# RWKV-7 recurrence feeding a hash-routed expert layer: GpSimd's products on VectorE and ScalarE, one masked read of k's scores, and the loads of decays on GpSimd's queue

## The chip, the cores and the metric

The kernel runs on one core of a Trainium2 chip. The core has five engines with a queue of instructions each: TensorE (PE, matrix products, with PEld for its weight loads), VectorE (DVE), ScalarE (ACT), GpSimd (POOL) and SyncE (SP, which here only issues DMAs). An engine works its queue in order, and an instruction that waits for another engine holds up all that stand behind it. Times are device microseconds of one execution, and the metric is the median of several executions.

## What is computed

A recurrence over 768 steps for 4 batches and 8 heads, with a state of 40 by 40 for each, and then a layer of 8 experts, of which each token uses one, given by its id:

```python
for t in range(S):                       # B=4, H=8, S=768, D=40
    y[:, :, t] = einsum('bhd,bhde->bhe', rt, state)
    Sa = einsum('bhde,bhe->bhd', state, at)
    state = state * wt[:, :, None, :] - einsum('bhd,bhe->bhde', Sa, bt)
    state = state + einsum('bhd,bhe->bhde', vt, kt)
x = y.transpose(0, 2, 1, 3).reshape(3072, 320)
e = token_ids * 2654435761 % 8           # the token's expert
out[token] = maximum(x[token] @ w1[e], 0) @ w2[e]
```

All values are float32.

## The kernel before, in words

**Tiles and ticks.** The recurrence is computed in chunks of C = 64 steps. A tile is one chunk of two batches with all 8 heads (rows 0 to 63 of the 128 partitions are one batch, 64 to 127 the other); there are 12 chunks and 2 pairs of batches, so 24 tiles `u`. Four tiles make a group, for which VectorE inverts small triangular blocks; 2 chunks (4 tiles) make a round of decays, and there are 6 rounds and 6 groups.

The order of work is written out by hand: each step is registered with a time in ticks (`at_tick`), all steps are sorted by it, and TensorE, VectorE, ScalarE and GpSimd get their instructions in that order. A tick is about one tile. Within a tick the steps have the order of the list `STEPS`: r1, at_t, z, c, y, r_t, sd, a, rc, x, s, v_t, r0, u. SP's order is left to the scheduler.

**Preparing a tile** (`tile_a`, at tick `u`). At `u - 1.0` SP loads the running products of the decays, `pl` and `ql`, from `p_rows` and `q_rows` in DRAM (4 DMAs), and the inputs `al` and `kb` (6 DMAs). At `u - 0.3` GpSimd multiplies `at = al * pl` (L371) and `z = kb * ql` for b and for k (L373, two operations). TensorE transposes `at` and `z` (`t_ps`, `z_ps`), ScalarE copies them back, and TensorE makes the scores `a_ps` in two banks of PSUM. Eight ScalarE copies take `a_ps` apart: `pk` (L413, L414) and `no` (L415) are scores of b, `mk` (L420) those of k, and GpSimd multiplies `mk` with the mask `after` in place (L422).

**Inverting a group** (`group_i`). When four tiles have their `pk`, VectorE transposes it to `nb` (L450), makes 31 pairs of an outer product and an addition (`outer` L459, `ub` L462) over three ticks, and transposes the result to `ut` and `ug` (L470, L471).

**Using a tile** (`tile_m`, `tile_s`, `tile_b`, eight ticks behind its preparation). The pieces that matter here: ScalarE and GpSimd fill `um` (GpSimd's half is L495, `ug` times the column `first`); TensorE makes `r_ps`, `c_ps`, `rc_ps`, `s_ps` and `y_ps`; VectorE masks `rc_ps` into `mr` (L603), scales the new state `st` (L625) and writes the output rows `xs` (L642), which GpSimd's queue stores to `x_rows` (L645). `py`, rows of `p_rows` again, is loaded by GpSimd's queue (L525).

**Decays** (`decays`). SP loads a round's w into `pb` (one buffer). VectorE makes running products forwards into `pb` (L277) and backwards into `qb` (L282), then `own`; TensorE exchanges halves with one small product `f_ps` (L293); VectorE makes `ends` and `rends`. GpSimd multiplies `pb` by `rends` (L311) and VectorE `qb` by `ends` (L317), each 128x1280, and SP stores them as `p_rows` and `q_rows`. The first two rounds are made ahead of the first tile; the later ones begin one tick before a group's four tiles are complete.

**Buffers.** `pl`, `al`, `ql`, `kb` have two buffers each, so a load for tile `u` waits until tile `u - 2` is multiplied. The double banks of PSUM (`two_banks`) are two, used in turn by z_ps, c_ps, sd_ps, a_ps, rc_ps, v_ps: `v_ps` gets the one that `a_ps` had, and the next `z_ps` the one that `rc_ps` had.

After the recurrence come the experts, which are not changed. The functions that the change touches:

## Time and profile before

| | |
|---|---|
| median of 3 runs | 925.74 us (922.95 to 933.06) |
| the profiled execution | 921.35 us, of which 919.6 us span |
| TensorE busy | 720.6 us (78%) |
| VectorE busy | 401.9 us (44%) |
| GpSimd busy | 297.2 us (32%) |
| ScalarE busy | 281.5 us (31%) |

The span is the time from the first to the last instruction in the trace. TensorE's clock is granted by the chip; a granted clock of 1.0 is 2.4 GHz, 0.5 is 1.2 GHz, and a number between is a stretch with both. Of an instruction the trace has its start, its duration, and, where the engine was idle before it, how long and what ended the wait.

### The profile page before, as it was taken

What the parts mean: (1) busy time and instruction counts of PE and PEld (TensorE: products, weight loads), DVE (VectorE), ACT (ScalarE), POOL (GpSimd) and SP (SyncE); (2) the same over time, 40 slices, a digit from 0 to 9 for tenths busy, and PEclk for the clock granted to TensorE, in tenths of its full rate; (3) what the DMA queues carried; (4) which work ended last, traced back from release to release, by engine and by line L of the source; (5) the groups of instructions that cost most, each with busy time, mean ns of one, the idle gap of its engine ahead of it and who ended that gap; (6) DMA issues with size and microseconds to landing.
All of it is one profiled execution on the core that took longest, in us unless ns stands there. A gap on an engine that the chain in (4) does not pass through costs nothing.

```text
span 919.6 us, 25403 instructions
## 1 busy us (share of the span) xinstructions
PE 720.6 (78%) x11032; PEld 503.3 (55%) x11032; DVE 401.9 (44%) x807; ACT 281.5 (31%) x634; POOL 297.2 (32%) x354
## 2 busy tenths in 40 slices
PE   0033344996998788989999929999999999999993
PEld 0022233885787677877888823536363636354542
DVE  8333799888856776586693211010110110110100
ACT  0024442664556365665644400000011011010000
POOL 4044434453545456546522232121221203020101
PEclk9985655996779698898998978999999999999997
DMA  4756385554876576653432163222222314130000
GB/s 78 147 103 127 69 166 107 95 130 97 125 129 91 93 114 106 101 111 63 51 75 54 40 220 96 72 93 78 86 88 79 130 38 153 46 113 1 21 8 16
DMA packets 208033, 83.03 MB, mean 90 GB/s; under 512 B 186926, under 2 KB 198191, under 8 KB 207920
## 3 DMA queue, kind: packets, MB, share of 16 engines
q1 hardware_dynamic: 201008, 64.32, 34.7%
q0 software_dynamic: 6912, 17.07, 6.5%
q8 instruction: 87, 1.43, 0.7%
q14 instruction: 26, 0.21, 0.1%
HBM read 65.58 MB, written 17.08 MB: 90 GB/s over the span
## 4 chain that ended last, share of the span: by engine, by line
PE 59%; issue 8%; POOL 6%; DVE 5%; DMA 3%; SPq 2%; ACT 0%; POOLq 0%; DVEq 0%
PE up_ps L831 21%; PE dn_ps L841 15%; PE y_ps L203 4%; PE z_ps L386 2%; PE nc_ps L203 2%; PE r_ps L203 2%; PE c_ps L203 2%; PE s_ps L203 2%; PE rc_ps L203 1%; PE u_ps L203 1%; POOL z L373 1%; POOL um L495 1%; PE t_ps L428 1%; PE xg_ps L821 1%; POOL at L371 1%
## 5 line engine op out<-in xcount | busy, mean ns | idle before, releaser
L831 PE MATMUL up_ps<-xt,w 128*128 128x512 f32 (+1 forms) x384 | 192.2, 631 | 8.6 <-issue 8.1
L841 PE MATMUL dn_ps<-w,ht 128*128 128x320 f32 x512 | 140.0, 434 | 0.0
L831 PEld LDWEIGHTS up_ps<-xt,w 128*128 128x128 f32 (+1 forms) x384 | 62.9, 189 | 133.7 <-issue 132.7
L841 PEld LDWEIGHTS dn_ps<-w,ht 128*128 128x128 f32 x512 | 96.6, 190 | 45.3 <-issue 6.1
L845 POOL DMA_INDIRECT out_dram<-o,idx_all x32 | 32.0, 1001 | 270.6 <-ACT o L844 265.5
L834 DVE TENSOR_SCALAR ht<-up_ps 128x512 f32<-128x512 f32 x32 | 22.1, 692 | 175.1 <-PE up_ps L831 139.2
L462 DVE TENSOR_TENSOR ub<-ub,outer 128x31 f32<-128x31 f32 (+15 forms) x186 | 92.3, 496 | 6.4
L459 DVE TENSOR_TENSOR outer<-ub,nb 128x31 f32<-128x31 f32 (+15 forms) x186 | 80.6, 433 | 4.5
L836 ACT ACTIVATE ht<-up_ps 128x512 f32<-128x512 f32 x32 | 19.1, 597 | 192.5 <-PE up_ps L831 163.0
L823 DVE COPY xt<-xg_ps 128x256 f32<-128x256 f32 x32 | 13.2, 413 | 128.2 <-PE xg_ps L821 128.2
L422 POOL TENSOR_TENSOR mk<-mk,after 128x512 f32<-128x512 f32 x24 | 32.0, 1332 | 112.2 <-ACT mk L420 95.2
L293 PE MATMUL f_ps<-own,partner 128*128 128x40 f32 x12 | 3.9, 424 | 81.4 <-DVE own L291 81.4
L645 POOL DMA_DIRECT2D x_rows<-xs x48 | 25.9, 544 | 116.4 <-DVE xs L642 69.6
L844 ACT COPY o<-dn_ps 128x320 f32<-128x320 f32 x32 | 13.6, 426 | 148.4 <-PE dn_ps L841 148.4
L428 PE MATMUL t_ps<-ident,at 128*104 128x128 f32 x96 | 21.0, 358 | 48.5 <-POOL at L371 48.5
L293 PEld LDWEIGHTS f_ps<-own,partner 128*128 128x128 f32 x12 | 3.0, 310 | 82.2 <-DVE own L291 82.2
L386 PE MATMUL z_ps<-ident,z 128*104 128x128 f32 x192 | 44.5, 401 | 3.9 <-POOL z L373 3.9
L373 POOL TENSOR_TENSOR z<-kb,ql 128x320 f32<-128x320 f32 x48 | 44.3, 941 | 0.0
L816 POOL DMA_INDIRECT xg<-x_rows,src_all x32 | 30.9, 967 | 35.5 <-PE xg_ps L821 18.6
L428 PEld LDWEIGHTS t_ps<-ident,at 128*104 128x104 f32 x96 | 13.0, 165 | 51.4 <-POOL at L371 50.9
L311 POOL TENSOR_TENSOR pb<-pb,rends 128x1280 f32<-128x1280 f32 x6 | 19.6, 3272 | 63.8 <-DVE rends L305 63.8
L386 PEld LDWEIGHTS z_ps<-ident,z 128*104 128x104 f32 x192 | 31.9, 187 | 12.8 <-POOL z L373 11.5
(153 smaller groups left out, 1239.0 us busy)
## 6 DMA issues: line engine op xcount, KB each, us to landing
w<-in_moe_w_dram SPq DMA_DIRECT2D x8, 1280.0 KB
w<-in_moe_w_dram SPq DMA_DIRECT2D x8, 1024.0 KB
ql<-q_rows SPq DMA_DIRECT2D x48, 160.0 KB
pb<-in_w_dram SPq DMA_DIRECT2D x24, 160.0 KB
al<-in_a_dram SPq DMA_DIRECT2D x48, 80.0 KB
kb<-in_b_dram SPq DMA_DIRECT2D x48, 80.0 KB
kb<-in_k_dram SPq DMA_DIRECT2D x48, 80.0 KB
r<-in_r_dram SPq DMA_DIRECT2D x48, 80.0 KB
```

The lines of the kernel that those rows point to most:

```text
L203: nc.tensor.matmul(out_, lhsT=lhsT, rhs=rhs, start=start, stop=stop, skip_group_check=True)
L373: nc.gpsimd.tensor_tensor(heads(x["z"][:, be]), view(x["kb"][:, be]), view(x["q"][:, be]), op=OP.mult)
L386: nc.tensor.transpose(p[0:R, be, hp * P:(hp + 1) * P], x["z"][:, be, hp, :], ident[:])
L422: nc.gpsimd.tensor_tensor(mk, mk, after[:].unsqueeze(1).to_broadcast([P, H, C]), op=OP.mult)
L428: nc.tensor.transpose(p[0:R, hp, :], src[:, hp, 0:R], ident[:])
L459: nc.vector.tensor_tensor(tv, ub[:, 0:j + 1, j:j + 1].to_broadcast([P, j + 1, m]), nb[:, j, j + 1:].unsqueeze(1).to_broadcast([P, j + 1, m ...
L462: nc.vector.tensor_tensor(o, o, tv, op=OP.add)
L645: nc.gpsimd.dma_start(x_rows[r0:r0 + C, :], xs[half(be), :])
L816: nc.gpsimd.indirect_dma_start(out=xg[:], out_offset=None, in_=x_rows[:], in_offset=bass.IndirectOffsetOnAxis(ap=idx, axis=0))
L831: nc.tensor.matmul(p[:], lhsT=w1[0:m, c, f * P:(f + 1) * P], rhs=xt[0:m, c, 0:n], start=(c == 0), stop=(c == 2))
L841: nc.tensor.matmul(p[:], lhsT=ht[:, f, j * P:(j + 1) * P], rhs=w2[:, f, :], start=(f == 0), stop=(f == FP - 1))
L845: st = nc.gpsimd.indirect_dma_start(out=out[:], out_offset=bass.IndirectOffsetOnAxis(ap=idx, axis=0), in_=o[:], in_offset=None, bounds_che ...
```

## The change

The products `at` and `z` of a tile, and the product of `pb` with `rends`, go from GpSimd to VectorE. GpSimd's half of `um` goes to ScalarE, as a copy with a scale. The columns of `a_ps` are arranged so that k's scores lie together for all rows: VectorE then reads them from PSUM, masks them and writes `mk` in one operation, and b's scores need four ScalarE copies instead of six. The loads of `pl` and `ql` are issued by GpSimd instead of SP. A tile's loads are placed at `u - 1.7` instead of `u - 1.0`, its products at `u - 0.7` instead of `u - 0.3`.

```diff
--- before.py
+++ after.py
@@ -308,7 +308,7 @@
         def _():
 
             p = segs(x["pb"])
-            nc.gpsimd.tensor_tensor(p, p, x["rends"][:].unsqueeze(2).to_broadcast([P, SEG, SL, D]), op=OP.mult)
+            nc.vector.tensor_tensor(p, p, x["rends"][:].unsqueeze(2).to_broadcast([P, SEG, SL, D]), op=OP.mult)
             store(0, x["pb"][:])
 
         @then.append
@@ -344,7 +344,7 @@
         ri, rn = divmod(n, RN)
         x = tiles[u]
 
-        @at_tick(u - 1.0)
+        @at_tick(u - 1.7)
         def _():
             x["p"] = pl = work.tile([P, DM], F32, tag="pl", name="pl")
             x["a"] = al = work.tile([P, DM], F32, tag="al", name="al")
@@ -355,22 +355,22 @@
                 return t.rearrange("t (h e) -> t h e", h=H)
             p_rows, q_rows = (d[rn * C:(rn + 1) * C] for d in pq_dram[ri])
             for be in range(2):
-                nc.sync.dma_start(pl[half(be)], of_batches(p_rows, 2 * g + be, 1))
-                nc.sync.dma_start(ql[half(be)], of_batches(q_rows, 2 * g, 2))
+                nc.gpsimd.dma_start(pl[half(be)], of_batches(p_rows, 2 * g + be, 1))
+                nc.gpsimd.dma_start(ql[half(be)], of_batches(q_rows, 2 * g, 2))
             load(lambda be, rows: by_head(al[rows]), a, 2 * g, n * C)
 
             load(lambda be, rows: by_head(kb[rows, be]), b, 2 * g, n * C)
             load(lambda be, rows: by_head(kb[rows, be]), k, 2 * g, n * C, crossed=True)
 
-        @at_tick(u - 0.3)
+        @at_tick(u - 0.7)
         def _():
             x["at"], x["z"] = at_r(u), z_r(u)
 
             def view(t):
                 return t.rearrange("p (hp two e) -> p hp two e", hp=HP, two=2)
-            nc.gpsimd.tensor_tensor(heads(x["at"]), view(x["a"][:]), view(x["p"][:]), op=OP.mult)
+            nc.vector.tensor_tensor(heads(x["at"]), view(x["a"][:]), view(x["p"][:]), op=OP.mult)
             for be in range(2):
-                nc.gpsimd.tensor_tensor(heads(x["z"][:, be]), view(x["kb"][:, be]), view(x["q"][:, be]), op=OP.mult)
+                nc.vector.tensor_tensor(heads(x["z"][:, be]), view(x["kb"][:, be]), view(x["q"][:, be]), op=OP.mult)
 
         @at_tick(u, "at_t")
         def _():
@@ -395,31 +395,26 @@
                 for be in range(2):
                     for i in range(2):
                         for par in range(2):
-                            c0 = (hp * 2 + be) * C
+
+                            c0 = ((i == be) * HP + hp) * C
                             mm(p[half(i), par, c0:c0 + C], x["z_t"][half40(par), be, hp, half(i)],
                                x["at_t"][half40(par), hp, be, :])
-
-            def scores(rows, be, c0, c1):
-
-                return p[rows].rearrange("p two (hp b t) -> p two b hp t", hp=HP, b=2)[:, :, be, :, c0:c1]
-
+            scores = p[:].rearrange("p two (kb hp t) -> p two kb hp t", kb=2, t=C)
+            of_b = scores[:, :, 1]
+
+            x["mk"] = mk = work.tile([P, 2, HP, C], F32, tag="mk", name="mk", bufs=LAG)
+            nc.vector.tensor_tensor(mk[:], scores[:, :, 0], after[:].unsqueeze(1).unsqueeze(1).to_broadcast([P, 2, HP, C]),
+                                    op=OP.mult)
 
             if ti == 0:
                 groups[gi]["pk"] = work.tile([P, GRP, 2, HP, BLK], F32, tag="pk", name="pk", bufs=1)
             pk = groups[gi]["pk"][:, ti]
             x["no"] = no = work.tile([P, 2, HP, BLK], F32, tag="no", name="no", bufs=LAG)
+            nc.scalar.copy(pk, of_b[:, :, :, 0:BLK])
             for be in range(2):
-                top, low = slice(be * C, be * C + BLK), slice(be * C + BLK, (be + 1) * C)
-                nc.scalar.copy(pk[top], scores(top, be, 0, BLK))
-                nc.scalar.copy(pk[low], scores(low, be, BLK, C))
-                nc.scalar.copy(no[top], scores(top, be, BLK, C))
-
-            x["mk"] = mk = work.tile([P, 2, HP, C], F32, tag="mk", name="mk", bufs=LAG)
-            for be in range(2):
-                rows = half(1 - be)
-                nc.scalar.copy(mk[rows], scores(rows, be, 0, C))
-            mk = mk[:].rearrange("p two hp t -> p (two hp) t")
-            nc.gpsimd.tensor_tensor(mk, mk, after[:].unsqueeze(1).to_broadcast([P, H, C]), op=OP.mult)
+                low = slice(be * C + BLK, (be + 1) * C)
+                nc.scalar.copy(pk[low], of_b[low, :, :, BLK:C])
+            nc.scalar.copy(no[:], of_b[:, :, :, BLK:C])
 
     def turn(t, src):
 
@@ -492,8 +487,8 @@
                 low = slice(be * C + BLK, (be + 1) * C)
                 nc.scalar.copy(xi[low, :, 0:BLK], p[low])
             x["um"] = um = work.tile([P, H, C], F32, tag="um", name="um")
-            nc.gpsimd.tensor_scalar(um[:, :, 0:BLK], groups[gi]["ug"][:, ti * H:(ti + 1) * H, :],
-                                    first[:, 0:1], None, op0=OP.mult)
+            nc.scalar.activation(um[:, :, 0:BLK], groups[gi]["ug"][:, ti * H:(ti + 1) * H, :], AF.Copy,
+                                 scale=first[:, 0:1])
 
         @at_tick(t0 - 1, "u")
         def _():
```

How this moves instructions shows at three places. First VectorE, at the program's start, from the second round's `rends` on. Before:

```order
L305 TENSOR_SCALAR rends<-rends 128x160
L317 TENSOR_TENSOR qb<-qb,ends 128x1280
L319 COPY qb<-ends 128x40
L264 TENSOR_SCALAR qb<-pb 128x1280
L265 SCALAR_TENSOR_TENSOR pb,wbad<-qb,pb 128x1280
```

After (at_84 and at_86 are the two buffers of `at`, z_102 and z_104 the first of ten of `z`; `mk` is L406 now):

```order
L311 TENSOR_TENSOR pb<-pb,rends 128x1280
L317 TENSOR_TENSOR qb<-qb,ends 128x1280
L319 COPY qb<-ends 128x40
L371 TENSOR_TENSOR at_84<-al,pl 128x4x2x40
L373 TENSOR_TENSOR z_102<-kb,ql 128x4x2x40 x2
L371 TENSOR_TENSOR at_86<-al,pl 128x4x2x40
L373 TENSOR_TENSOR z_104<-kb,ql 128x4x2x40 x2
L406 TENSOR_TENSOR mk<-a_ps,after 128x512
L371 TENSOR_TENSOR at_84<-al,pl 128x4x2x40
L373 TENSOR_TENSOR z_106<-kb,ql 128x4x2x40 x2
```

The products of tiles 0 and 1 stand directly behind the second round, and those of tile 1 ahead of the mask of tile 0.

Second GpSimd, in two ticks with all kinds of work. Before:

```order
L422 TENSOR_TENSOR mk<-mk,after 128x512
L495 TENSOR_SCALAR um<-ug,first 128x8x32
L371 TENSOR_TENSOR at_84<-al,pl 128x4x2x40
L373 TENSOR_TENSOR z_102<-kb,ql 128x4x2x40 x2
L525 DMA py<-p_rows 64x320 x2
L645 DMA x_rows<-xs 64x320 x2
L422 TENSOR_TENSOR mk<-mk,after 128x512
```

After:

```order
L358 DMA pl<-p_rows 64x320
L359 DMA ql<-q_rows 64x640
L358 DMA pl<-p_rows 64x320
L359 DMA ql<-q_rows 64x640
L520 DMA py<-p_rows 64x320 x2
L640 DMA x_rows<-xs 64x320 x2
```

The arithmetic is gone, and four more DMAs are issued for each tile.

Third VectorE, where a later round of decays meets the start of a group (from the fifth round's `L277` to its `own`; other rows between are the routing of tokens). Before:

```order
L642 SCALAR_TENSOR_TENSOR xs<-y_ps,py 128x320
L277 TENSOR_TENSOR pb<-pb,qb 128x4x40 x2
L282 TENSOR_TENSOR qb<-qb 128x4x40 x4
L743 CAST eidf<-eid 128x24
```

After:

```order
L637 SCALAR_TENSOR_TENSOR xs<-y_ps,py 128x320
L277 TENSOR_TENSOR pb<-pb,qb 128x4x40
L371 TENSOR_TENSOR at_84<-al,pl 128x4x2x40
L373 TENSOR_TENSOR z_106<-kb,ql 128x4x2x40 x2
L277 TENSOR_TENSOR pb<-pb,qb 128x4x40
L282 TENSOR_TENSOR qb<-qb 128x4x40 x4
L406 TENSOR_TENSOR mk<-a_ps,after 128x512
L738 CAST eidf<-eid 128x24
```

`at` and `z` of the next tile and the mask of this one stand in the middle of the decays, ahead of `nb` and `own`.

## Rows read from the trace of the kernel before

**Rows 1.** Stretches: length, busy time by engine (instructions), granted clock, DMA share, GB/s.

```profile
54.50:97.00 42.50, 17.91 (x304) 13.51 (x304) 8.00 (x18) 18.26 (x42) 16.64 (x18) 0.67 0.69 134
97.00:143.40 46.40, 20.63 (x343) 16.30 (x343) 44.13 (x78) 18.92 (x46) 19.01 (x17) 0.56 0.61 114
...
170.50:218.60 48.10, 41.53 (x1304) 37.23 (x1302) 43.71 (x97) 34.00 (x77) 24.33 (x31) 0.97 0.70 138
218.60:298.50 79.90, 68.56 (x1699) 60.90 (x1699) 56.05 (x113) 39.72 (x92) 38.88 (x44) 0.78 0.65 104
298.50:376.20 77.70, 64.58 (x1707) 57.65 (x1708) 52.43 (x93) 41.72 (x97) 41.40 (x47) 0.82 0.63 108
376.20:444.40 68.20, 60.76 (x1697) 53.35 (x1694) 45.42 (x81) 41.33 (x92) 38.36 (x46) 0.90 0.46 84
```

The engines stand in the order PE, PEld, DVE, ACT, POOL.

**Rows 2.** Timeline of the first tile: start, duration, engine, line, operation, tiles [idle before].

```profile
54.53 0.85 POOL L371 TENSOR_TENSOR at<-al,pl 128x320 f32<-128x320 f32 x1
...
55.43 1.09 PE L428 MATMUL t_ps<-ident,at 128*104 128x128 f32 x4 [6.01 <-POOL at L371]
...
60.51 0.36 ACT L413 COPY pk<-a_ps 32x256 f32<-32x256 f32 x1 [1.16 <-PE a_ps L203]
...
63.89 1.26 POOL L422 TENSOR_TENSOR mk<-mk,after 128x512 f32<-128x512 f32 x1 [6.87 <-ACT mk L420]
...
65.11 0.86 POOL L371 TENSOR_TENSOR at<-al,pl 128x320 f32<-128x320 f32 x1
```

**Rows 3.** Timeline of VectorE: the output rows of two tiles in turn.

```profile
182.55 0.49 DVE L642 SCALAR_TENSOR_TENSOR xs<-y_ps,py 128x320 f32<-128x320 f32 x1
...
196.62 0.49 DVE L642 SCALAR_TENSOR_TENSOR xs<-y_ps,py 128x320 f32<-128x320 f32 x1
```

**Rows 4.** Timeline of TensorE: three waits, the last one of a round of decays.

```profile
365.26 0.65 PE L428 MATMUL t_ps<-ident,at 128*104 128x128 f32 x4 [1.17 <-POOL at L371]
...
360.84 0.43 PE L540 MATMUL v_ps<-ident,x 64*104 64x64 f32 x8 [0.56 <-ACT mk L420]
...
223.47 0.65 PE L293 MATMUL f_ps<-own,partner 128*128 128x40 f32 x2 [6.96 <-DVE own L291]
```

**Rows 5.** Groups by line, 40 to 540 us: count, busy us, mean ns, idle before.

```profile
L373 POOL TENSOR_TENSOR z<-kb,ql 128x320 f32<-128x320 f32 x48 | 44.3, 941 | 0.0
...
L603 DVE TENSOR_TENSOR mr<-rc_ps,after 128x1024 f32<-128x1024 f32 x24 | 29.3, 1220 | 19.2 <-PE rc_ps L203 19.2
...
L645 POOL DMA_DIRECT2D x_rows<-xs x48 | 25.9, 544 | 116.4 <-DVE xs L642 69.6 <-DVE outer L459 40.8 <-DVE pb L277 6.1
```

**Rows 6.** Timelines of GpSimd and VectorE: the first two rounds of decays.

```profile
20.38 4.05 POOL L311 TENSOR_TENSOR pb<-pb,rends 128x1280 f32<-128x1280 f32 x1 [12.62 <-DVE rends L305]
...
21.61 2.86 DVE L319 COPY qb<-ends 128x40 f32<-128x40 f32 x1
...
50.34 1.48 DVE L317 TENSOR_TENSOR qb<-qb,ends 128x1280 f32<-128x1280 f32 x1
```

**Rows 7.** Timeline: GpSimd's `um`, and VectorE's operation that begins beside it.

```profile
346.77 0.95 POOL L495 TENSOR_SCALAR um<-ug,first 128x256 f32<-128x256 f32 x1
...
346.90 3.50 DVE L459 TENSOR_TENSOR outer<-ub,nb 128x192 f32<-128x192 f32 x1
```

**Rows 8.** Stretches, instructions of L459, then of L462: groups 0, 2 and 5.

```profile
97.00:143.40 46.40, 15.30 (x31) 0.56 0.61 114
...
218.60:288.00 69.40, 12.82 (x31) 0.77 0.64 102
...
444.40:484.70 40.30, 10.89 (x31) 1.00 0.40 62
...
97.00:143.40 46.40, 17.52 (x31) 0.56 0.61 114
...
218.60:288.00 69.40, 16.36 (x31) 0.77 0.64 102
...
444.40:484.70 40.30, 11.51 (x31) 1.00 0.40 62
```

## The prediction

> **What bounds the kernel now.** I read first the busy time by stretch [rows 1], cut where the kernel's own stages begin. What follows 444.4 us, the last ticks and the expert layer, prepares no new tiles, and the change hardly touches it. Before that, three things follow one another.
>
> In the first 54.5 us the decays of two rounds are made, one after the other, and nothing else can start. From 54.5 to 97 us the first tiles are prepared at one per 10.58 us (`at` of tile 0 starts at 54.53, of tile 1 at 65.11 [rows 2]), while every engine is less than half busy. The rows show why: GpSimd makes `at`, TensorE transposes from 55.43, ScalarE's eight copies start at 60.51, GpSimd masks `mk` at 63.89, and only then takes `at` of the next tile, because its queue holds them in that order. It is one serial loop through four engines. From 97 to 143.4 us VectorE is the bound: it is busy 44.13 of 46.4 us with the first group's block inversion [rows 1].
>
> Then the recurrence runs, four tiles to a group, and the three stretches of 79.9, 77.7 and 68.2 us are four ticks each [rows 1]. No engine is full in them: VectorE is busy 56.05 of 79.9 us. TensorE is busy 68.56 us, but at a granted clock of 0.78 (a mixture of its levels 1.2 and 2.4 GHz); 68.56 times 0.78 is 53.5, and the same product is 53.0 and 54.7 in the next two stretches. So about 54 us per group is what TensorE needs at 2.4 GHz, and a good tick shows it: between two `xs` rows, 182.55 and 196.62, lie 14.07 us [rows 3], or 56.3 per group. The other 12 to 24 us per group are TensorE's waits and the lower clock behind them. The waits are of three kinds [rows 4]: at the head of a tile for GpSimd's `at` (1.17 us), before `v_ps` for ScalarE's copies of `mk` out of PSUM (0.56 us), and once per round for VectorE's decays (`f_ps`, 6.96 us).
>
> **The change part by part.** *VectorE's new work.* Per tile it gets one `at`, two `z` and one `mk`. The trace has no such operation on VectorE; the nearest is `xs`, 128x320, 0.49 us [rows 3], and for `mk` from PSUM the masking `mr`, twice as large, 1.22 us [rows 5], so 0.65 with some fixed cost. That is 3 times 0.49 plus 0.65, or 2.1 us per tile (bounds: 1.8, were all priced by size at `mr`'s rate, and 4.0, were the three to cost GpSimd's 0.94 [rows 5] and `mk` as much as `mr`). I take 2.1, since `xs` has the same shape. Per round it also gets the product with `rends`, 128x1280, whose twin `L317` takes 1.48 us [rows 6]. Per group: 4 times 2.1 plus 1.5, or 9.9 us.
>
> *What VectorE gets back.* While GpSimd computes, VectorE stalls: with `um` (and `at` and `z` behind it) on GpSimd from 346.77 us, one 128x192 product took 3.50 us [rows 7], and a 128x40 copy under GpSimd's 4.05 us product took 2.86 us [rows 6]. The block inversion's 62 operations take 15.30 + 17.52 = 32.8 us in group 0 and 12.82 + 16.36 = 29.2 in group 2, but 10.89 + 11.51 = 22.4 in the last group, where no `at`, `z` and `mk` are left [rows 8]. So 10.4 us come back in group 0 and about 7 in a later one. By the Trainium skill ("SBUF — State Buffer", Who interferes with whom) a VectorE instruction with two SBUF inputs and a GpSimd instruction that reads SBUF block one another for whole instructions. The trace agrees in the 3.50 us row, and by that rule all of the stretching ends, since what GpSimd keeps are memsets and DMA issues. Net, a later group costs VectorE some 3 us more: 59, where TensorE needs 56.3.
>
> *Start.* The product with `rends` moves from 4.05 us on GpSimd to 1.48 on VectorE, ahead of `L317`. GpSimd's product of the first round ends at 20.38 + 4.05 = 24.43 now, VectorE's would at 21.86 [rows 6]; so the stores, the next load, which the store must free a buffer for, and the second round move up by 2.6 us. `L317` of that round starts at 50.34 now [rows 6], so VectorE has the two products done at 47.74 + 1.48 + 1.48 = 50.7, and with 0.2 allowed for the copy behind them starts `at` of tile 0 at 50.9 instead of 54.53. Gain: 3.6 us.
>
> *First tiles.* By the order of VectorE, `at` and `z` of tile 1 now stand ahead of `mk` of tile 0, so the loop is cut. A tile then costs what TensorE and ScalarE need in a row: 60.51 less 55.43, or 5.1 us (lower bound 20 us for four); the upper bound is the 42.5 us of now. Between them stands the DMA work of this stretch: 0.69 of 42.5 us is 29 us of all DMA engines [rows 1], and the loads are the same. I take 29. Gain: 13.5 us.
>
> *First group.* 46.4 us, less 10.4 of stalls, plus 1.5 and three tiles at 2.1: 43.8. Gain: 2.6 us.
>
> *From 143.4 to 218.6* an `f_ps` wait stays, since VectorE is as full ahead of it as before, and the ticks behind it, from 170.5 us on, run at a granted clock of 0.97 already [rows 1]. Gain: 0, give or take 4.
>
> *Groups from 218.6 on.* `at` comes about half a tick earlier, on an engine that has time, so the 1.17 us wait ends, and with it the clock loss that follows. What is late next is `f_ps`: on VectorE `nb`, the rest of the decays and `own` stand in line as before, now with `at`, `z` and `mk` ahead of them. I keep 7 us for it and 7 us for the half clock behind it: 56.3 + 14 = 70 in the two groups that hold decays, and 58.5 in the third, which has none. Gains: 10, 7.7 and 9.7 us.
>
> *Costed at nothing.* ScalarE's copies out of `a_ps` fall from eight to four per tile and `um` comes to it; by its busy share of about half in the groups [rows 1] both are covered. Loading `pl` and `ql` from GpSimd takes four of SP's loads per tile away and puts four issues of 0.54 us [rows 5] where GpSimd's arithmetic stood; they start 0.7 tick earlier. Behind them on GpSimd stand `py` and the stores of `x_rows`, both needed a tick later. If that cover fails, rival (d) prices it.
>
> Sum: 3.6 + 13.5 + 2.6 + 0 + 10 + 7.7 + 9.7 = 47.1 us. The profiled execution took 921.35 us (span 919.6), which gives 874.3; the median of the runs, 925.74, is 4.4 higher, which gives 878.7. I say 877, and put the rivals on the same footing, some 2.5 above the profiled execution's.
>
> **The rivals.** (a) *TensorE's floor everywhere*: without GpSimd's stalls VectorE reaches `own` in time, so the 14 us of wait and half clock go in two groups (28 more), the third group gains 2 more, and the first tiles run at 5.1 us each (8.5 more): about 838. For it: VectorE idles over 20 us in each of those stretches. Against: the `f_ps` wait comes from a burst, not from the mean.
>
> (b) *VectorE in order takes most of it back*: `mk` now waits on VectorE for `a_ps`, with the inversion queued behind it, and `v_ps` takes `a_ps`'s PSUM buffer, so a late `mk` holds TensorE. If the later groups keep their 79.9, 77.7 and 68.2 us, only the start's 19.7 us are gained: about 904.
>
> (c) *Slower*: the same hold, but large. If VectorE's lag reaches `v_ps` by some 7 us in every tick, the size of the `f_ps` wait, TensorE falls to half clock each time and all ticks run as in the worst group, 20 us. The three groups then cost 3 times 79.9 less 225.8, or 14 more, and the 48.1 us from 170.5 on, three ticks of 16 us, 12 more; less the start's 19.7, that is 6 slower than now: about 930, and over 1% where the clock stays low between. It decides from a lag of 7 us per tick. Against: VectorE's mean of 59 in 70 us leaves it room to recover.
>
> (d) *No net change, loads late*: GpSimd now issues about ten DMAs per tick. If each had to wait for a VectorE operation, as the copy of 2.86 us waited for GpSimd [rows 6], ten times 0.54 + 2.86 is 34 us per tick, over twice the tick; a third of such waits would already use up the gain: about 923. Against: few VectorE operations are copies. The Trainium skill ("SBUF — State Buffer", SBUF: two separate sides) warns of just this: GpSimd cannot write a DMA's descriptors during a two-port VectorE copy. No row here shows a DMA issue so delayed.
>
> **How the numbers follow.** My forecast 0.47 (858 to 898), (a) 0.15 (830 to 858), (b) 0.22 (898 to 914), (d) 0.08, (c) 0.08. Faster by over 1%, about what a measurement of this kernel can tell from no change, holds the first three: 0.84; within 1% 0.08; slower 0.08. The range 845 to 910 leaves out (c), (d), the best of (a) and the worst of (b); the bounds of VectorE's price, -0.3 and +1.9 us for each of 24 tiles, -7 and +46 were all of it on the path, lie inside it but for the far end.
>
> **What would show it.** After: `at` of tile 1 close behind `z` of tile 0, `nb` of group 0 near 80 us and its last transposition back near 124; inversion operations at some 22 us per group all over; the wait for `at` before `t_ps` gone; ticks of 14 to 15 us in the last full group. Wrong if `v_ps` waits for VectorE's `mk` by over 2 us per tick, if `at` waits for `pl` or `ql`, or if the granted clock in the groups stays at 0.8.

## The result and the profile after

The changed kernel takes 898.94 us (median; 894.51 to 918.71), the kernel before 924.35 beside it: a ratio of 0.969, interval 0.962 to 0.976. The profiled execution took 894.51 us, its span 892.7 instead of 919.6. The forecast of 877 us had the direction and the start, and nearly twice the gain. Of two kernels below (a_noload and b_noload) only one execution of four was undisturbed, so only medians and the lowest times are told of them, and their traces, like that of a_pool_mask, are of disturbed executions. The same stretches as in [rows 1], from the windows of the changed kernel (the columns are those of [rows 1]), cut at the same events (`at` of tile 0, `nb` of group 0, end of the first inversion, first `mr`, `nb` of groups 2 to 5, last `xs`):

```profile
0.00:50.80 50.80, 2.10 (x6) 1.21 (x6) 33.38 (x74) 2.21 (x9) 11.94 (x37) 1.00 0.60 109
50.80:84.20 33.40, 20.30 (x304) 16.77 (x304) 15.51 (x37) 11.68 (x27) 11.40 (x22) 1.00 0.96 189
84.20:123.70 39.50, 20.78 (x343) 17.74 (x343) 37.45 (x91) 11.68 (x30) 4.12 (x8) 0.82 0.76 131
123.70:151.70 28.00, 15.09 (x317) 13.42 (x314) 23.67 (x61) 9.88 (x25) 7.96 (x16) 0.58 0.58 110
151.70:203.60 51.90, 46.88 (x1304) 43.03 (x1302) 42.92 (x109) 27.58 (x63) 13.57 (x26) 0.87 0.55 113
203.60:277.40 73.80, 60.49 (x1699) 55.07 (x1699) 55.78 (x129) 36.21 (x84) 25.05 (x40) 0.88 0.73 119
277.40:349.80 72.40, 62.33 (x1705) 56.73 (x1707) 49.60 (x110) 36.52 (x84) 25.84 (x42) 0.84 0.66 110
349.80:415.90 66.10, 60.09 (x1702) 54.32 (x1699) 42.78 (x94) 36.05 (x80) 24.81 (x38) 0.92 0.51 78
415.90:511.90 96.00, 89.81 (x2680) 82.43 (x2676) 49.04 (x103) 45.06 (x98) 16.09 (x32) 0.91 0.25 49
```

Set against the forecast (us gained; before less after):

| stretch | before | after | gained | forecast |
|---|---|---|---|---|
| to `at` of tile 0 | 54.5 | 50.8 | 3.7 | 3.6 |
| first tiles | 42.5 | 33.4 | 9.1 | 13.5 |
| first group | 46.4 | 39.5 | 6.9 | 2.6 |
| to `nb` of group 2 | 75.2 | 79.9 | -4.7 | 0 |
| three groups | 225.8 | 212.3 | 13.5 | 27.4 |
| to the last `xs` | 91.9 | 96.0 | -4.1 | 0 |
| expert layer | 383.3 | 380.8 | 2.5 | 0 |
| span | 919.6 | 892.7 | 26.9 | 47.1 |

The first three rows sum to 19.7 in both columns, but that agreement is partly luck: the first tiles gained 4.4 less than forecast and the first group 4.3 more. Of the 20.2 us that are missing in the end, 13.9 lie in the three groups and 8.8 in the two stretches around them; the 2.5 of the expert layer, which was not changed, go the other way.

What the forecast asked the trace to show is mostly there. In the timeline of VectorE and ScalarE, `at` of tile 1 stands close behind `z` of tile 0, where [rows 2] had 10.58 us from one `at` to the next; then tile 2 waits for its load:

```profile
50.84 0.48 DVE L371 TENSOR_TENSOR at<-al,pl 128x320 f32<-128x320 f32 x1
51.24 0.89 DVE L373 TENSOR_TENSOR z<-kb,ql 128x320 f32<-128x320 f32 x2
52.05 0.48 DVE L371 TENSOR_TENSOR at<-al,pl 128x320 f32<-128x320 f32 x1
...
57.25 0.69 DVE L406 TENSOR_TENSOR mk<-a_ps,after 128x512 f32<-128x512 f32 x1 [3.92 <-PE a_ps L203]
57.98 0.37 ACT L413 COPY pk<-a_ps 128x256 f32<-128x256 f32 x1 [2.62 <-DVE mk L406]
...
63.70 0.49 DVE L371 TENSOR_TENSOR at<-al,pl 128x320 f32<-128x320 f32 x1 [5.75 <-DMA al<-in_a_dram]
```

`nb` of group 0 stands at 84.2 us (forecast: near 80) and its last transposition ends near 123.7 (near 124). The prices are those of the forecast: 0.48 us for `at`, 0.45 for each `z`, 0.69 for `mk`, 2.06 per tile against the 2.1 taken. The last row but one holds what no step had foreseen: ScalarE's copy of b's scores waits for VectorE's `mk`, since both read the tile `a_ps` and `mk` is written first.

The inversion's operations fall to 21.1 us in every group, 10.5 plus 10.6 (forecast: some 22; [rows 8] had 32.8, 29.2 and 22.4), here grouped by line from 203.6 to 266.5 us:

```profile
L457 DVE TENSOR_TENSOR ub<-ub,outer 128x31 f32<-128x31 f32 (+15 forms) x31 | 10.6, 343 | 1.1
L454 DVE TENSOR_TENSOR outer<-ub,nb 128x31 f32<-128x31 f32 (+15 forms) x31 | 10.5, 340 | 0.6
```

What did not come are ticks of 14 to 15 us all through the last full group: its `mr` rows stand 17.5, 16.2, 15.0 and 17.5 us apart. Of the signs that the forecast named for being wrong, `v_ps` does not wait for `mk`, and `at` waits for `al` and not for `pl` or `ql`; the granted clock in the groups, 0.88, 0.84 and 0.92, rose from 0.78, 0.82 and 0.90, but in the second group little.

**Where the gain of the groups went.** In the three groups TensorE is busy 182.9 of 212.3 us. Busy time times granted clock, row by row, is 160.9 us, and 161.1 before: TensorE's work at full clock, unchanged. The rest is idle time (29.4 now, 31.9 before) and what the half clock costs, busy time less that product (22.0 now, 32.8 before). So the idle time hardly fell; of the 13.5 us gained, 10.8 are half clock. TensorE's waits show why; first the kernel before, 218.6 to 444.4 us, then the changed one, 203.6 to 415.9 (us in total, times, longest):

```profile
PE f_ps L293 <- DVE own L291: 14.2, 2, 7.2
PE t_ps L428 <- POOL at L371: 8.0, 9, 1.4
PE s_ps L203 <- issue: 4.1, 4, 1.4
...
PE z_ps L386 <- POOL z L373: 2.0, 9, 0.3
```

```profile
PE f_ps L293 <- DVE own L291: 11.9, 2, 6.5
PE s_ps L203 <- issue: 4.8, 4, 2.2
PE x_ps L203 <- issue: 4.1, 2, 2.5
PE y_ps L203 <- issue: 3.0, 2, 1.8
...
```

The waits for GpSimd's `at` and `z`, 10 us, are gone as forecast. In their place stand more stops put down to "issue", in which TensorE waits for nothing that the profile shows: 17.3 us in all instead of 9. Most stand in the middle of a stream of equal matmuls, as here (timeline of TensorE):

```profile
169.16 0.54 PE L203 MATMUL u_ps<-ug,xi 32*64 32x32 f32 x12
170.68 0.92 PE L203 MATMUL u_ps<-ug,xi 32*64 32x32 f32 x20 [0.98 <-issue]
...
239.38 0.62 PE L203 MATMUL s_ps<-x,z 128*40 128x40 f32 x21
242.16 0.43 PE L203 MATMUL s_ps<-x,z 128*40 128x40 f32 x11 [2.16 <-issue]
```

Windows cut from the end of one stop to the end of a later one (the first number with an x counts matmuls) give them a pattern:

```profile
165.65:170.67 5.02, 4.04 (x128) 3.55 (x127) 4.85 (x11) 3.30 (x8) 1.55 (x4) 1.00 0.68 178
170.67:186.59 15.92, 14.61 (x381) 13.57 (x382) 10.88 (x35) 8.49 (x19) 4.15 (x8) 0.79 0.46 99
236.95:242.15 5.20, 3.04 (x127) 2.75 (x128) 4.99 (x12) 2.55 (x7) 4.59 (x9) 1.00 1.03 216
242.15:259.08 16.93, 15.25 (x382) 14.04 (x381) 10.16 (x28) 7.91 (x18) 5.53 (x9) 0.80 0.98 141
352.18:380.21 28.03, 25.94 (x637) 23.71 (x637) 17.53 (x45) 14.01 (x30) 7.03 (x11) 0.82 0.58 90
```

The counts are 1, 3, 1, 3 and 5 times 128, less one or a few. With its weight loads a block of 128 matmuls is 256 instructions. Counted so, 15.0 of the 17.3 us lie between two blocks; the rest are shorter stops elsewhere, the longest 0.86 us. The DMA queue of the instructions, in the page of the same kernel, fits that:

```profile
q8 instruction: 87, 1.43, 0.7%
```

These are 87 packets of 16.4 KB, and 11032 matmuls with 11032 weight loads make 86.2 blocks of 256. I read a stop as TensorE having used up one block of instructions before the next is there. The times of these packets bear that out: between 150 and 510 us TensorE makes twelve stops of 0.88 us or more, and each ends 1.32 to 1.62 us after such a packet has landed, where the packets start 5.0 us apart in the mean. Where two stops lie one block apart (165.66, 236.96 and 310.40 us to the next), the packet between them starts 2.5, 2.7 and 1.4 us after the block's first matmul, lands at 3.7, 3.7 and 3.2 us, and TensorE goes on at 5.0, 5.2 and 4.7 us, though it was busy with the block for only 4.0, 3.0 and 2.2 us. The kernel before has the stops too (128 matmuls from 258.92 to 263.84 us, and from 409.34 to 413.81).

The half clock begins mostly behind such stops, or in a wait. Between 150 and 510 us nine stretches at half clock begin, by windows of half a microsecond; seven begin in a stop of 0.88 us or more or up to 2 us behind its end, the other two (205 and 277 us) in the waits for `f_ps`, the first of these 2.2 us behind a stop. Four stops of over 1 us (270.95, 300.09, 342.99 and 380.22 us) were followed by none. Around the stop that ends at 242.16:

```profile
240.00:242.20 2.20, 0.04 (x3) 0.04 (x4) 2.13 (x5) 2.10 (x6) 1.90 (x4) 1.00 1.09 215
242.20:244.20 2.00, 2.00 (x37) 1.71 (x37) 1.92 (x5) 0.70 (x2) 0.89 (x1) 0.66 1.82 187
244.20:246.20 2.00, 2.00 (x38) 1.94 (x38) 1.80 (x6) 0.09 (x1) 0.00 (x0) 0.50 1.06 62
...
248.20:250.20 2.00, 2.00 (x16) 1.77 (x15) 0.00 (x0) 0.78 (x2) 0.00 (x0) 0.64 0.53 59
250.20:252.20 2.00, 2.00 (x80) 1.95 (x81) 0.00 (x0) 1.92 (x4) 0.00 (x0) 1.00 1.05 237
```

TensorE idles 2.2 us, then runs seven at a granted clock of about 0.5, that is at 1.2 GHz, and then is back at 2.4. So this stop of 2.2 us costs some 5.5 us with the half of the seven.

### The profile page after: what moved, and what is told of

Its sections match the earlier page's. It is cut to its first block, busy times and chain, and to the rows that moved or that the text cites. A ratio compares the mean times of both kernels' runs of the same rounds, so it can differ in the third digit from the quotient of the medians.

```text
span 892.7 us, 25236 instructions
## 1 busy us (share of the span) xinstructions
PE 722.1 (81%) x11032; PEld 511.7 (57%) x11032; DVE 392.2 (44%) x909; ACT 249.6 (28%) x562; POOL 204.5 (23%) x324
## 2 busy tenths in 40 slices
DMA packets 204192, 83.02 MB, mean 93 GB/s; under 512 B 186926, under 2 KB 195119, under 8 KB 204080
## 4 chain that ended last, share of the span: by engine, by line
PE 73%; DVE 12%; issue 5%; DMA 5%; SPq 2%; ACT 1%; POOL 0%; DVEq 0%; POOLq 0%
PE up_ps L826 22%; PE dn_ps L836 16%; PE r_ps L203 5%; PE y_ps L203 4%; PE s_ps L203 4%; PE u_ps L203 3%; PE rc_ps L203 3%; PE t_ps L423 3%; PE nc_ps L203 2%; PE a_ps L203 2%; PE z_ps L386 2%; PE c_ps L203 2%; PE sd_ps L648 2%; PE x_ps L203 2%; DVE qb L282 1%
## 5 line engine op out<-in xcount | busy, mean ns | idle before, releaser
L457 DVE TENSOR_TENSOR ub<-ub,outer 128x31 f32<-128x31 f32 (+15 forms) x186 | 63.8, 343 | 6.3
L454 DVE TENSOR_TENSOR outer<-ub,nb 128x31 f32<-128x31 f32 (+15 forms) x186 | 63.2, 340 | 3.8
L203 PE MATMUL a_ps<-at_t,z_t 40*64 40x64 f32 x1536 | 36.4, 247 | 12.7 <-ACT z_t L388 11.1
L637 DVE SCALAR_TENSOR_TENSOR xs<-y_ps,py 128x320 f32<-128x320 f32 x24 | 11.8, 491 | 72.4 <-PE y_ps L203 70.0
L203 PEld LDWEIGHTS a_ps<-at_t,z_t 40*64 40x64 f32 x1536 | 30.8, 156 | 20.2 <-ACT z_t L388 16.2
L358 POOL DMA_DIRECT2D pl<-p_rows x48 | 25.8, 537 | 69.7 <-DVE at L371 43.8
L386 PE MATMUL z_ps<-ident,z 128*104 128x128 f32 x192 | 36.7, 355 | 0.7 <-DVE z L373 0.7
L203 PE MATMUL r_ps<-x,mk 64*64 64x40 f32 x768 | 33.0, 249 | 1.0 <-issue 0.9
L598 DVE TENSOR_TENSOR mr<-rc_ps,after 128x1024 f32<-128x1024 f32 x24 | 29.1, 1215 | 10.3 <-PE rc_ps L203 10.3
```

The source lines that it names most:

```text
L203: nc.tensor.matmul(out_, lhsT=lhsT, rhs=rhs, start=start, stop=stop, skip_group_check=True)
L358: nc.gpsimd.dma_start(pl[half(be)], of_batches(p_rows, 2 * g + be, 1))
L386: nc.tensor.transpose(p[0:R, be, hp * P:(hp + 1) * P], x["z"][:, be, hp, :], ident[:])
L454: nc.vector.tensor_tensor(tv, ub[:, 0:j + 1, j:j + 1].to_broadcast([P, j + 1, m]), nb[:, j, j + 1:].unsqueeze(1).to_broadcast([P, j + 1, m ...
L457: nc.vector.tensor_tensor(o, o, tv, op=OP.add)
L598: nc.vector.tensor_tensor(t[:].rearrange("p two h t -> p (two h) t"), p[:].rearrange("p two (h t) -> p (two h) t", t=C), after[:].unsqueez ...
```

## The experiments

Every ratio is to the kernel before, run on the same chip beside it; the changed kernel's is 0.969 (0.962 to 0.976).

**1. The order alone, on GpSimd (b_order).**

```diff
 # the kernel before
-        @at_tick(u - 1.0)        # loads of a tile
+        @at_tick(u - 1.7)
-        @at_tick(u - 0.3)        # at and z
+        @at_tick(u - 0.7)
```

> The kernel before with two numbers changed: a tile's loads are issued at tick u - 1.7 instead of u - 1.0, and its at and z are made at u - 0.7 instead of u - 0.3. All arithmetic stays on GpSimd, which now makes at and z of the next tile ahead of mk of this one. Theory 'order': the first tiles were slow because GpSimd's queue closed a loop through four engines, so cutting the loop alone gives most of the 9 us that the stretch of the first tiles gained (42.5 to 33.4): 915 us, and nb of group 0 near 88 us instead of 96.9. Theory 'engine': GpSimd's own 4.9 us per tile and its stalls of VectorE are the matter: no change, 922 to 926. In both the 62 inversion operations of group 0 stay near 33 us.

Measured: 928.98 us, ratio 1.001 (0.996 to 1.007). The start does gain: `at` of tile 0 starts at 51.72 and of tile 1 at 54.17, and `nb` of group 0 stands at 89.89 instead of 96.92. By the first `mr` 8.4 us of it are left (162.09 for 170.53), two ticks later none (200.08 for 199.85). The inversion costs VectorE 29 to 34 us in groups 0 to 4, since GpSimd's `at` and `z` still run under it. In the groups TensorE's waits for `at` are gone by the order alone, but its stops are 18.0 us there and its wait for `f_ps` 17.8. Both theories were half right: the order opens the loop, and without the other engine nothing of it reaches the end.

**2. The engine alone, in the old order (a_late).**

```diff
 # the changed kernel
-        @at_tick(u - 1.7)
+        @at_tick(u - 1.0)
-        @at_tick(u - 0.7)
+        @at_tick(u - 0.3)
```

> The changed kernel with the old ticks: loads at u - 1.0, at and z at u - 0.3, so that VectorE makes them behind mk of the tile before and the loop of the first tiles is closed again, with VectorE in GpSimd's place. Theory 'order and engine each bring a part of the start': the first tiles take about 40 us instead of 33, and the groups wait for at as before: 908 to 914. Rival 'the engine alone': VectorE's 2 us per tile instead of GpSimd's 5 keep the loop short, 897 to 902.

Measured: 897.64 us, ratio 0.957 (0.950 to 0.963). The engine alone does it; the interval lies a little below the changed kernel's and all but clear of it, so the new order brings nothing that shows. The waits for `at` in the groups are gone here too, and the stops are 15.0 us. The loop is closed again, as the timeline of VectorE shows, but it takes 7.0 us now:

```profile
57.49 0.48 DVE L371 TENSOR_TENSOR at<-al,pl 128x320 f32<-128x320 f32 x1
...
63.90 0.69 DVE L406 TENSOR_TENSOR mk<-a_ps,after 128x512 f32<-128x512 f32 x1 [5.12 <-PE a_ps L203]
64.51 0.48 DVE L371 TENSOR_TENSOR at<-al,pl 128x320 f32<-128x320 f32 x1
```

That is no longer the bound: `nb` of group 0 stands at 83.05 us, with the loop open at 84.22. By their share, 0.96 in the changed kernel and 0.98 here, the DMA engines bound the stretch in both; no run made its loads lighter.

**3. `at` and `z` back on GpSimd, in the new order (a_pool_atz).**

```diff
-            nc.vector.tensor_tensor(heads(x["at"]), ...)     # and z
+            nc.gpsimd.tensor_tensor(heads(x["at"]), ...)
```

> The changed kernel with at and z back on GpSimd, everything else, the order too, as changed. Theory 'GpSimd stalls VectorE': the inversion operations, 21 us per group now, grow to some 26 us wherever at and z lie under them (groups 0 to 4), the first group's stretch grows by 4 to 5 us and f_ps comes later: about 908. Rival 'VectorE's load counts': VectorE is freed of 1.5 us per tile and at and z have time on GpSimd, so 895 to 899.

Measured: 916.89 us, ratio 0.987 (0.969 to 1.005). This interval touches the changed kernel's, so the times alone leave it open; the trace does not. The start keeps its gain (`nb` of group 0 at 82.50), the three groups lose all of it: 234.2 us instead of 212.3. VectorE's operations grow where the theory had them, to 27.6 us in group 2 (by line, 202.8 to 272.5 us):

```profile
L457 DVE TENSOR_TENSOR ub<-ub,outer 128x31 f32<-128x31 f32 (+15 forms) x31 | 15.8, 509 | 1.1
L454 DVE TENSOR_TENSOR outer<-ub,nb 128x31 f32<-128x31 f32 (+15 forms) x31 | 11.8, 381 | 0.6
```

`f_ps` then waits 9.22 us instead of 5.34 in that group, and 4.92 instead of 6.52 in the next. TensorE idles only 3.3 us more in the three groups; what doubles is its loss to the half clock, 43.8 us for 22.0. So that VectorE's operations stretch under `at` and `z` is shown, and that TensorE loses its clock with it in this one execution; how the one leads to the other is not. The stretching agrees with the rule of the Trainium skill ("SBUF — State Buffer", Who interferes with whom) that the prediction weighed.

**4. The mask back on ScalarE and GpSimd (a_pool_mask).**

```diff
-            nc.vector.tensor_tensor(mk[:], scores[:, :, 0], after..., op=OP.mult)
+            for be in range(2):
+                nc.scalar.copy(mk[half(1 - be)], ...)        # and six copies of pk and no
+            nc.gpsimd.tensor_tensor(mk, mk, after..., op=OP.mult)
```

> The changed kernel with the masking of k's scores as before: ScalarE copies mk out of a_ps in pieces (eight copies per tile again) and GpSimd masks it in place; at, z, um, the product with rends, the ticks and the loads as changed. Theory 'every GpSimd operation that reads SBUF under the inversion costs VectorE': one operation per tile of about 1.3 us instead of the three of at and z, so a third to a half of the 18 us that at and z cost: 905 to 908, the inversion at 23 to 24 us per group. Rival 1: ScalarE's eight copies hold v_ps up too, 912 or more. Rival 2: the copies wait for TensorE alone and not for VectorE, so 890 to 897.

Measured: 918.76 us, ratio 0.972 (0.963 to 0.982), which cannot be told from the changed kernel's. The inversion takes 23.2 us per group with a mask under it, as the theory had it; whether the mask alone is worth time stays open.

**5. `pl` and `ql` by SP's queue (a_spload).**

```diff
-                nc.gpsimd.dma_start(pl[half(be)], ...)       # and ql
+                nc.sync.dma_start(pl[half(be)], ...)
```

> The changed kernel with pl and ql loaded through SP's queue again, at the new tick u - 1.7. Theory 'who issues is indifferent': 895 to 903. Rival 1, 'GpSimd's issues are slow' (its own waits for xs stand ahead of them): faster, 885 to 893. Rival 2, 'on SP's queue they hold up what stands behind them' (SP waits for the stores of p and q there): the first tiles slow down, 905 to 912.

Measured: 908.52 us, ratio 0.971 (0.964 to 0.979), not to be told from the changed kernel's. In the trace `nb` of group 0 stands at 87.68 instead of 84.22: a small part of rival 2, no more.

**6. ScalarE's copies ahead of `mk` (a_swap).**

```diff
-            nc.vector.tensor_tensor(mk[:], ...)              # ahead of the copies
             nc.scalar.copy(pk, ...)                          # and three more
+            nc.vector.tensor_tensor(mk[:], ...)
```

> The changed kernel with mk on VectorE written behind ScalarE's four copies out of a_ps, so that the copies wait for TensorE alone and mk waits for them. Theory 'copies behind mk': ScalarE's 79.3 us of waits for mk hold um, xi and x_t behind them and with them TensorE; then each group gains 2 to 4 us and the whole about 886 to 890, the waits of 'pk' for VectorE being gone. Rival: ScalarE has the time, or VectorE's new wait takes it back: 899 give or take 4.

Measured: 907.63 us, ratio 0.980 (0.963 to 0.997). In the changed kernel ScalarE's waits before `pk` are (40 to 510 us):

```profile
ACT pk L413 <- DVE mk L406: 79.3, 24, 9.4
```

They are gone here and no time with them. The interval is 3.4% wide; it leaves out the 886 to 890 us of the theory by little, and a smaller gain it can't exclude.

**7. `f_ps` later (a_fps).**

```diff
-            p = bank([P, D], "f_ps")                         # at the end of the step that makes own
-            nc.tensor.matmul(p, lhsT=partner[:], rhs=own[:, 0], ...)
+        @at_tick(t0 + span + (0.65 if ri >= 2 else 0.0), order=8)
+        def _():                                             # the same matmul
-        decays(ri, t0, 0.7, t0 + 1.0, 0.3)
+        decays(ri, t0, 0.7, t0 + 1.4, 0.3)
```

> The changed kernel with the f_ps matmul of rounds 2 to 5 taken out of the step that makes own and put 0.66 tick later in the program (the steps that follow it 0.4 tick later), so that TensorE doesn't stand before it while VectorE is still on own. Nothing is left out. Theory 'f_ps and the half clock behind it': the waits of 5.34 and 6.52 us go and with them some 7 us each of half clock: 24 to 26 us, about 874; the waits of 10.37 and 12.91 lie in the start where VectorE is the bound, so they bring 0 to 5 more. Rival 'gaps in TensorE's own issue hold the clock down whatever it waits for': a part of the wait comes back elsewhere and the clock in these groups stays below 0.9: 890 to 899.

Measured: 899.59 us, ratio 0.970 (0.951 to 0.989), not to be told from the changed kernel; the 874 us of the theory lie outside. The waits of 5.34 and 6.52 us are gone from the rounds; in the trace the three groups take 214.2 us instead of 212.3, with 7 us less idle time and some 8 more lost to the half clock. TensorE's waits from 200.8 to 415 us:

```profile
PE s_ps L203 <- issue: 6.1, 4, 2.0
PE v_ps L537 <- ACT no L419: 5.1, 3, 3.1
```

With `f_ps` out of its way TensorE runs into `v_ps`, whose PSUM buffer `a_ps` still holds: ScalarE has not copied it, for it waits for VectorE's `mk`. That is the prediction's rival (b), in the place of the wait that was taken away. The rest is the stops, 18.3 us where they were 17.3.

**8 and 9. Lighter loads (a_rows, b_rows).** The same edit in both kernels.

```diff
-                src[b0 + be, :, t0:t0 + C, :].rearrange("h t e -> t h e")
+                src[b0 + be, (t0 // C) % H, 0:C * H, :].rearrange("(t h) e -> t h e", h=H)   # a, b, k of tiles 8 to 23
```

> The changed kernel, in which the loads of a, b and k for tiles 8 to 23 read 64 contiguous rows of 1280 bytes from one head instead of 8 heads times 64 rows of 160 bytes: the same bytes to the same places, an eighth of the packets; the values loaded are other ones, all else is unchanged. Theory 'late instructions': in the groups TensorE stops in the middle of a stream, always a multiple of 128 matmuls after its last such stop, because its next block of instructions comes late through busy DMA engines, and each stop of over 1 us is followed by about 7 us at half clock. With the DMA engines eased these stops fall from 17.4 us to under 8 in the three groups from nb of group 2 to nb of group 5, the half-clock loss from 22 us to about 10, and some 8 more come from the stretches around: 865 to 875. Rival 'waits for VectorE and ScalarE hold the groups': they are untouched, so 891 to 899.

> The same contiguous loads of a, b and k for tiles 8 to 23 in the kernel before. Theory 'late instructions': the stops in the groups are 9 us there, the waits for at and f_ps 25 us, so easing the DMA engines brings less than in the changed kernel, 8 to 15 us: 910 to 918, and the change is then worth 40 us or more between the two kernels with eased loads. Rival: the loads matter alike or not at all, and the change is worth the same 25 us between them.

Measured: 901.36 us, ratio 0.970 (0.964 to 0.976), and 927.59, ratio 0.998 (0.994 to 1.002). Neither moved by anything that shows. The edit was weak: the packets of the whole run fall from 204192 to 161184, but the DMA share in the three groups only from 0.73, 0.66 and 0.51 to 0.67, 0.59 and 0.50. The stops are 14.2 us.

**10 and 11. Most loads left out (a_noload, b_noload).** The same edit in both kernels.

```diff
+            if u >= 10:                                      # tiles 10 to 23: the data of tile u - 2
+                for key in ("p", "a", "q", "kb"):
+                    x[key] = tiles[u - 2][key]
+                return
...
+            if u < 10:
                 load(... x["r"] ...)
```

> The changed kernel without the loads of p, a, q, b, k and r for tiles 10 to 23: these tiles use the data of the tile two before, so the values are other ones and 12 of the 18 loads and stores per tile are gone from the fourth tick before the groups on; every arithmetic instruction stays. Theory 'late instructions through busy DMA engines': with the DMA share in the groups at a third of what it was, TensorE's stops at multiples of 128 matmuls fall from 17 us in the three groups to under 6 and the half-clock loss behind them from 22 to under 10; 865 to 872. Rival 'the stops do not come from the loads': stops and loss stay within 4 us of what they were, 893 to 899.

> The same leaving out of the loads for tiles 10 to 23 in the kernel before. Theory 'late instructions through busy DMA engines': the stops, 9 us there, go too, but the 25 us of waits for at and f_ps stay and keep the half clock behind them: 905 to 912, so that the change is worth 38 us or more between the two kernels without loads, near the 47 of the forecast. Rival: both kernels keep their times and the difference stays at 25.

Measured: 902.35 and 922.27 us (before: 937.14), 19.9 apart; the lowest times are 884.56 and 908.17. The times decide little; what the traces count does more. This edit was strong. The windows of the three groups of a_noload:

```profile
198.90:270.20 71.30, 61.02 (x1702) 55.57 (x1699) 55.65 (x129) 36.35 (x85) 18.63 (x26) 0.88 0.51 65
270.20:344.30 74.10, 61.78 (x1681) 56.55 (x1683) 49.50 (x111) 36.58 (x85) 18.46 (x27) 0.86 0.43 47
344.30:409.60 65.30, 61.58 (x1724) 56.42 (x1722) 42.60 (x94) 36.09 (x81) 17.22 (x25) 0.87 0.29 33
```

They moved 65, 47 and 33 GB/s (last column), not 119, 110 and 78, and took 210.7 us instead of 212.3; the stops are 14.2 us, the loss to the half clock 24. In b_noload the stops are 9.1 us, where the kernel before has 9. So the tile loads are not what makes most of the stops, and the half of the theory that blamed busy DMA engines falls.

**12. Three edits at once (a_late_fps_swap).** The edits of 2, 6 and 7.

```diff
+ loads at u - 1.0, at and z at u - 0.3        (as a_late)
+ mk behind ScalarE's copies of a_ps           (as a_swap)
+ f_ps 0.66 tick later, ends 0.4 tick later    (as a_fps)
```

> The changed kernel with three edits at once: the old ticks (loads at u - 1.0, at and z at u - 0.3), the f_ps matmul 0.66 tick later, and mk written behind ScalarE's copies from a_ps. Each alone gave no clear loss or gain. Theory 'f_ps and v_ps cover each other': taking the f_ps wait alone let TensorE run into v_ps, which waits for ScalarE's copies behind VectorE's mk; without both, the 11.8 us of waits in the three groups go and the half clock behind them: 875 to 883. Rival 'late instructions': TensorE then stops at its multiples of 128 matmuls as often, 893 to 900.

Measured: 882.61 us, ratio 0.945 (0.937 to 0.954), clearly below the kernel before, and its interval lies below the changed kernel's. It overlaps that of experiment 2 (0.950 to 0.963), which has one of the three edits. In the groups its `f_ps` and `v_ps` waits are gone, and in their place `t_ps` waits for `at` again, with the old order (TensorE, 196 to 404.7 us):

```profile
PE t_ps L425 <- DVE at L373: 5.8, 4, 2.1
PE r_ps L203 <- issue: 4.9, 4, 2.5
...
```

and of its stretches the one before the groups, the first group and the one behind them:

```profile
133.80:196.00 62.20, 53.53 (x1589) 48.67 (x1587) 58.41 (x149) 35.61 (x82) 15.06 (x30) 0.91 0.65 125
196.00:269.00 73.00, 65.70 (x1684) 59.77 (x1681) 55.75 (x130) 35.58 (x84) 25.23 (x42) 0.81 0.83 118
...
404.70:496.80 92.10, 85.26 (x2673) 78.84 (x2667) 48.96 (x104) 43.99 (x96) 16.32 (x32) 0.96 0.27 52
```

Against the changed kernel 15.2 us of span are gained: 8.3 between `nb` of groups 1 and 2 (70.5 there), the stretch in which TensorE had stood 12.91 us before `f_ps`; 3.6 in the three groups (73.0, 68.7 and 67.0 us); 3.9 behind them, where TensorE loses 3.4 us to the half clock instead of 8.1. The time is the one that the theory named, but not by its account: in the three groups half clock and stops take most of it back. Idle time there falls by 8 us to 21.3, the loss to the half clock rises by 2.6 to 24.6, and the stops are 15.1 us, near as many as in the changed kernel. And of the 8.3 us ahead of the groups the trace of experiment 2 has 5.6 (64.9 us between the same two rows), though TensorE stands there 10.88 us before `f_ps`. No run has the edits of 6 and 7 without the old order, so how much each of the three brings is not shown.

## Why the forecast was right and wrong, step by step

- **What bounds the kernel**: right in its three parts. The product of busy time and clock, the forecast's 54 us per group, held in each kernel with an unchanged recurrence that was profiled (51 to 56 us).
- **VectorE's price and what it gets back**: right. 2.06 us per tile for 2.1; the inversion at 21.1 us. Experiments 3 and 4 show that the cause was named rightly: 27.6 us with GpSimd's `at` and `z` back under it, 23.2 with its mask. The mean was too high, though: VectorE is busy 55.8, 49.6 and 42.8 us per group, not 59. The 59 had been worked out from the fullest group alone, where 56.05 stood before (52.43 and 45.42 in the others), and the inversion gave back 8 us there and not 7.
- **Start**: right, 3.7 for 3.6.
- **First tiles**: size off (9.1 for 13.5). By their share the DMA engines are the bound, as assumed, but the step "the loads are the same" failed: 0.69 times 42.5 is 29 us of DMA work before, 0.96 times 33.4 is 32 us now, since at 134 and 189 GB/s [rows 1, and the table above] the stretch moved 5.7 MB then and 6.3 now. That the new order cuts the loop was true and not needed (experiment 2).
- **First group**: undersized, 6.9 for 2.6. The sum had taken 46.4 less 10.4 and added the products and three tiles of new work to the path; VectorE's busy time there fell from 44.13 to 37.45 us, as much as the stretch. The inversion gave back 11.7 (10.4 in the sum), and operations of the decays that the sum had left as they were shrank too: the two at L282 from 1.4 to 0.6 us, the copy at L289 from 0.7 to 0.2. A rest of some 1.5 us I can't place. It is this miss that makes up for the one before it in the sum of 19.7.
- **Groups from 218.6 on**: here the forecast failed. The step is "Gains: 10, 7.7 and 9.7 us", built as 56.3 for TensorE plus 14 for `f_ps` and its half clock. The wait for `at` went, as it said. But the good tick of 14.07 us, taken as what TensorE needs, is a tick with a single stop of 0.37 us in it. The profile of before showed 9 us of "issue" in these groups, and the sum had no term for them; once TensorE no longer waited for `at`, they grew to 17.3 us, and to 18.0 and 15.0 us in the two kernels that lose the wait by the order alone or the engine alone (experiments 1 and 2). Beside them stands half clock that the sum had not: 22.0 us for the 14 that it had put behind the two `f_ps` waits. Of its six falls in the groups two lie in those waits, four in or close behind stops. The last group, without decays, gained 2.1 instead of 9.7, with no wait but stops in it.
- **The 14 us of `f_ps`**: the wait stayed, 11.9 us for the 14 of before, but it was no term by itself: without it (experiment 7) no gain shows, because `v_ps`, the stops and more half clock stand behind it.
- **143.4 to 218.6 and the end of the recurrence**: taken at 0, together they cost 8.8 us. In the end of the recurrence TensorE's loss to the half clock rose from 3.4 to 8.1 us, behind a stop of 0.88 us at 420.56. In the other stretch the ticks had a granted clock of 0.97 before [rows 1] and have 0.87 now. The other kernels with the change's engines take 62.2 to 68.5 us between `nb` of groups 1 and 2 where the changed one takes 70.5, so part of this loss may belong to the one execution that was profiled.
- **The rivals**: the number, 898.94, lies on the border between the forecast's own band and (b)'s, by 0.94 us in the latter, which says little of either. Of (b), the start's 19.7 us came out, and its mechanism is in the trace, as ScalarE's copies waiting for `mk`, but the groups did not keep their times, and `mk` held TensorE only in experiments 7 (5.1 us at `v_ps`) and 3 (5.7 us), not in the changed kernel. (a) fell with the stops. (c) and (d) did not appear: `v_ps` waits under 1 us at a time, and who issues `pl` and `ql` makes no difference that can be measured.

**What stays open**: why, at the three places above, the next packet starts only 1.4 to 2.7 us after a block has begun, and why TensorE goes on only some 1.4 us after it has landed. Taking away half of what the DMA engines moved in the groups left 14.2 of 17.3 us of stops. That the stops are instruction supply rests on their places (multiples of 128 matmuls), on the count of packets and on the times at which these land; no run changed the blocks themselves, so what the changed kernel would take without stops is not measured. Whether a stop is followed by half clock, four of twelve were not, is not explained either, and it makes a few microseconds in each stretch a matter of chance from one execution to the next.

## What to carry to other kernels

A wait that is taken off an engine with stops of its own can pay less than its length: sum first what the same engine loses to "issue" in the same stretch, and don't take the best tick as its floor. Here even that sum (9 us) would have been too low, since the stops grew to 15 to 18 us when the wait went. What VectorE gets back when arithmetic leaves GpSimd can be priced from the same operations in a stretch where GpSimd has none: 22.4 us there, 21.1 measured. Where two waits stand one behind the other, take away both before judging either: alone neither `f_ps` nor `mk` showed a gain, and both together with the old order took 15.2 us off the span, of which the old order may have brought a part.

## What the runs showed of the hardware that I had not expected

TensorE's stops without a releaser lie, but for the shortest, at multiples of 128 matmuls with their weight loads, 256 instructions, and the instruction queue moved 87 packets of 16.4 KB for 86.2 such blocks. Each of twelve stops ended 1.32 to 1.62 us after one of these packets had landed. A stop of 0.9 to 2.5 us was mostly followed by half clock, for 3.5 to 17.5 us, and so cost more than itself. Moving fewer bytes by other DMAs at that time hardly changed them.
